# A SwiGLU feed-forward layer on one core: the order and the shape of the first weight loads, and the order of the first matmuls

## The chip, the cores and the metric

The kernel runs on one core of a Trainium2 chip, in one launch. The metric is the time of one execution on the device in microseconds (us). Before the change it is 120.17 us, the median of three runs (119.89 to 120.64). The profile is one further execution, in which the hardware profiler recorded every instruction and every DMA packet.

## What is computed

One sequence of S = 2048 tokens of width D = 512 goes through a gated feed-forward layer with F = 1376 inner columns. All tensors are bf16.

```python
def reference(x, w_gate, w_up, w_down):
    g = _silu(x @ w_gate)
    u = x @ w_up
    return (g * u) @ w_down
```

x is [1, 2048, 512], w_gate and w_up are [512, 1376], w_down is [1376, 512].

## The kernel before

**Tiling.** D is cut into KD = 4 blocks of 128 rows (index dk), which are summed in PSUM. F is cut into ten tiles of 128 columns (ft 0 to 9) and a rest of 96 columns. The tokens are cut into NSC = 4 chunks of SC = 512. The hidden activations are kept transposed, with F on the partitions: for each chunk c and each tile ft there is a group "G" (gate) and a group "U" (up), and each of them fills one PSUM bank of 128 x 512. A group has four steps, one for each dk (`gu_step`), and each step is two matmuls of 64 weight columns, one for the upper and one for the lower half of the array's columns, which run side by side. ScalarE then writes the silu of the gate bank to an fp32 buffer `sg_sb` (four buffers), and VectorE multiplies that with the up bank into `hT_sb`. The rest of F is done in groups "X" (32 of its columns as gate and up, and further 64 as gate) and "Y" (those 64 as up). The second product, groups "O", runs over all tiles of F at the end, mostly in strips of 32 rows (`strips`), and its results are stored tile by tile.

**Order on the engines.** Every engine runs a list that is written out by hand. `plan_tiles` puts gates and ups in the order in which TensorE runs them: for each list in `fts` first all its gates, then all its ups; before the change these lists are [0], [1], [2, 3], [4], ... [9] in every chunk. `s_P` counts the groups that TensorE has finished, in that order, and ScalarE and VectorE wait for these counts. Eight banks are used in turn (`turn` says in which order), so a group waits (`free`) until those who read the group eight places before it are done.

**The opening.** TensorE starts with N_WARM = 6 matmuls of ones, 512 columns wide (`warm`, L359), and N_FILL = 2 fillers (L364), each of two matmuls of 64 rows and 128 columns. Then it waits for `xn`, the first 256 tokens as they lie in memory, and transposes them against the identity matrix (L374, L382). The four results, one for each dk, are copied to `xT_sb` by VectorE and ScalarE in turn. After that come the first gates and ups of chunk 0. The first 256 tokens are taken first (columns 0 to HT = 256 of the bank), since tokens 256 to 511 come later by two transposing DMAs, `x0b` and `x0c`. The order by hand is: gates of tiles 0 and 1 (alternating, dk by dk) and ups of tiles 0 and 1 on 256 tokens; gate 0 on the next 128 and the last 128; then up 0, gate 1 and up 1 on tokens 256 to 511. From tile 2 on a group runs on all 512 tokens at once.

**Loads.** `load_w` (L97) loads columns f0 to f1 of w_gate or w_up for all four dk in one DMA. The columns go by slabs of two tiles, (0, 2), (2, 4), (4, 6), (6, 8), and the last one, (8, 11). A row of such a DMA is 512 bytes long (256 columns), and the last slab's is longer. The slab of gates 0 and 1, `wg0`, is issued from ScalarE's queue (`loads_on_scalar`, L110); all others go from SyncE's queue in this order (`loads_on_sync`, L113): `xn`, `wu0` (ups 0 and 1), `x0b`, `x0c`, then gate and up of each further slab, `wut` (the last 32 columns of w_up), the transposing loads of chunks 1 to 3, w_down (`wd`), four copies of the last 96 rows of w_down on 32 partitions each (`wdt0` to `wdt3`), and `wdl`. A step of TensorE waits for the load that it needs first (`need`), each load having a semaphore of its own.

Of the kernel before, what the change touches and what calls it, by code (L numbers as in the profile page):

```python
# [6 lines left out]
BF16 = mybir.dt.bfloat16  # L7
FP32 = mybir.dt.float32

N_WARM = 6  # L10
N_FILL = 2


def bass_standalone__swiglu_ffn__prompt_kernel(nc, x, w_gate, w_up, w_down, out):
    _, S, D = x.shape
    F = w_gate.shape[1]
    P = 128
    KD = D // P
    NFF = F // P
    NFT = NFF + 1  # L20
# [26 lines left out]
    with ExitStack() as es:  # L47
# [17 lines left out]
        o_sb = [sb(f"o_sb{i}", [P, D], BF16) for i in range(NOS)]  # L65
        psum = ps("psum", [P, NB, 512], FP32)
        banks = [psum[:, i, :] for i in range(NB)]
        turn = [0, 2, 1, 3, 4, 5, 6, 7]

        xn_sb = sb("xn_sb", [P, NXN, D], BF16)  # L70
        ident = sb("ident", [P, P], BF16)
# [22 lines left out]
                xT_sb[:, :, t0:t1], xf[t0:t1, :]  # L94
            ).then_inc(load_sem(name), 16)

        def load_w(eng, name, src, base, f0, f1):  # L97
            eng.dma_start(
                w_sb[:, :, base + f0:base + f1],
                src[:, f0:f1].rearrange("(k p) f -> p k f", p=P),  # L100
            ).then_inc(load_sem(name), 16)

        slabs = [(0, 2), (2, 4), (4, 6), (6, 8), (8, NFT)]
        slab_of = {ft: a for a, b in slabs for ft in range(a, b)}

        def load_slab(eng, a, b):
            load_w(eng, f"wg{a}", w_gate, 0, a * P, min(b * P, F))
            load_w(eng, f"wu{a}", w_up, UPH, a * P, min(b * P, F - 32))

        def loads_on_scalar(act):  # L110
            load_w(act, "wg0", w_gate, 0, 0, slabs[0][1] * P)

        def loads_on_sync(sp):  # L113
            sp.dma_start(
                xn_sb[:, :, :].rearrange("p j d -> p (j d)"), xf[0:HT, :].rearrange("(p j) d -> p (j d)", j=NXN)
            ).then_inc(load_sem("xn"), 16)
            load_w(sp, "wu0", w_up, UPH, 0, slabs[0][1] * P)
            load_x(sp, "x0b", HT, HT + P)
            load_x(sp, "x0c", HT + P, SC)
            for a, b in slabs[1:]:  # L120
                load_slab(sp, a, b)
            load_w(sp, "wut", w_up, F - (F - 32), F - 32, F)
            for c in range(1, NSC):
                load_x(sp, f"x{c}", c * SC, (c + 1) * SC)
            sp.dma_start(
                wd_sb[:, 0:NFF, :], w_down[0:NFF * P, :].rearrange("(k p) d -> p k d", p=P)
            ).then_inc(load_sem("wd"), 16)
            for c in range(NSC):
                sp.dma_start(
                    wdt_sb[R * c:R * (c + 1), :, :], w_down[NFF * P:F, :].rearrange("(q p) d -> p q d", p=R)  # L130
                ).then_inc(load_sem(f"wdt{c}"), 16)
            sp.dma_start(wdl_sb[:, :], w_down[NFF * P:F, LASTA:D]).then_inc(load_sem("wdl"), 16)


# [94 lines left out]
        NT = len(groups)  # L229

        for c in range(NSC):
            for fts in [[0], [1], [2, 3]] + [[ft] for ft in range(4, NFF)]:
                plan_tiles(c, fts)
            plan_x(c)
        for pi in range(NSC // 2):
# [40 lines left out]
            ).then_inc(s_I, 1)  # L276

        def on_scalar(act):
            loads_on_scalar(act)
            act.activation(adummy[:, 0:4], zero_c, ACT.Silu)  # L280
            for op in act_ops:
                act.wait_ge(s_P, op["g"]["at"] + 1)
                if op["kind"] == "silu":
                    if op["free"]:
                        act.wait_ge(s_D, op["free"])
                    fn = ACT.Silu
                else:
                    if op["stored"][1]:
                        act.wait_ge(*op["stored"])
                    fn = ACT.Copy  # L290
                act.activation(op["out"], op["src"], fn).then_inc(s_A, 1)  # L291
            for t, c0, c1, ob, eng, n in stores:
                if (c0, c1) == (0, LASTA):
                    act.wait_ge(s_A, n)
                    act.dma_start(rows_of(t)[:, c0:c1], o_sb[ob][:, c0:c1]).then_inc(s_out[ob], 16)
# [16 lines left out]
        def on_tensor(pe):  # L312
# [19 lines left out]
            def gu_step(g, dk, n0, n1):  # L332
                c, ft = g["c"], g["ft"]
                if c > 0:
                    need(f"x{c}")
                if c == 0 and n1 > HT:
                    need("x0b")
                if c == 0 and n1 > HT + P:
                    need("x0c")
                need(("wg" if g["kind"] == "G" else "wu") + str(slab_of[ft]))  # L340
                if c == 0 and n0 < HT:
                    after(*xt_ready[dk])
                col = (0 if g["kind"] == "G" else UPH) + ft * P
                for m in (0, HC):
                    ins = pe.matmul(  # L345
                        g["bank"][m:m + HC, n0:n1], lhsT=w_sb[:, dk, col + m:col + m + HC],
                        rhs=xT_sb[:, dk, c * SC + n0:c * SC + n1], start=(dk == 0), stop=(dk == KD - 1),
                        tile_position=(0, m),
                    )
                if n1 == SC and dk == KD - 1:  # L350
                    ins.then_inc(s_P, 1)
# [30 lines left out]
                    ins = pe.transpose(tview_last()[m:m + HC, i, :], xn_sb[:, i, c0:c0 + HC], ident[:, :])  # L382
            ins.then_inc(s_P, 1)

            g0, u0, g1, u1 = groups[NT:NT + 4]
            for dk in range(KD):
                for g in (g0, g1):
                    gu_step(g, dk, 0, HT)
            for g in (u0, u1):
                gu_matmuls(g, 0, HT)  # L390
            gu_matmuls(g0, HT, HT + P)
            gu_matmuls(g0, HT + P, SC)
            for g in (u0, g1, u1):
                gu_matmuls(g, HT, SC)

            for g in groups[NT + 4:]:
                kind = g["kind"]
                if kind == "O":
                    break
                free(g)  # L400
                if kind in "GU":
                    gu_matmuls(g, 0, SC)
                elif kind == "X":
                    c = g["c"]
                    need(f"wg{slab_of[NFF]}")
                    need("wut")
                    for dk in range(KD):
                        for m in (0, HC):
                            ins = pe.matmul(  # L409
                                g["bank"][m:m + HC, :], lhsT=w_sb[:, dk, XC0 + m:XC0 + m + HC],  # L410
                                rhs=xT_sb[:, dk, c * SC:(c + 1) * SC],
                                start=(dk == 0), stop=(dk == KD - 1), tile_position=(0, m),
                            )
                    ins.then_inc(s_P, 1)
                elif kind == "Y":
                    need(f"wu{slab_of[NFF]}")
                    for dk in range(KD):
                        for c in (2 * g["pi"], 2 * g["pi"] + 1):
                            y0, y1 = yblk(c)
                            ins = pe.matmul(  # L420
                                g["bank"][y0:y1, :], lhsT=w_sb[:, dk, YC0:YC0 + 64],
                                rhs=xT_sb[:, dk, c * SC:(c + 1) * SC],
                                start=(dk == 0), stop=(dk == KD - 1),
                                tile_position=(0, y0), skip_group_check=True,
                            )
                    ins.then_inc(s_P, 1)
# [119 lines left out]
```

## Time and profile before

| | us |
|---|---|
| median of three runs | 120.17 |
| lowest and highest run | 119.89, 120.64 |
| the profiled execution | 120.67 |
| its span, first to last instruction | 119.3 |
| TensorE busy within the span | 116.6 |
| VectorE busy | 43.4 |
| ScalarE busy | 35.5 |
| SyncE's DMA queue, share of 16 engines | 27.1% |

The span is shorter than the execution's own time by 1.3 us, which lie before the first and behind the last instruction. Busy times of TensorE are to be read with care: a matmul's record runs from its start until its last result is written, so records of neighbours overlap, and a busy engine isn't one at full rate. How many matmuls of a shape start within a stretch tells the rate. A "DMA issue" is the instruction on the queue of SyncE (SPq) or ScalarE (ACTq); the time to landing counts from there to the last increment of the load's semaphore. The stretch that the change touches looks like this in the page's 40 slices of about 3 us each, from the left (tenths of busy time, then GB/s of all DMAs):

```
PE   7999999999999999999999999999999999999993
DVE  0103534442534452444352444369800040214331
ACT  4225243265242365232454323470000030213001
DMA  3999999991000000000000000000000023023612
GB/s 80 278 283 335 194 253 228 269 295 23 0 5 0 0 0 0 5 0 5 0 5 0 0 0 0 5 0 0 5 0 5 0 86 95 0 92 106 204 44 88
```

All weights and tokens are loaded in the first 29 us or so; the stores come at the end.

### The profile page before, as it was taken

What the parts mean: (1) busy time and instruction counts of PE and PEld (TensorE: products, weight loads), DVE (VectorE), ACT (ScalarE), POOL (GpSimd) and SP (SyncE); (2) the same over time, 40 slices, a digit from 0 to 9 for tenths busy, and PEclk for the clock granted to TensorE, in tenths of its full rate; (3) what the DMA queues carried; (4) which work ended last, traced back from release to release, by engine and by line L of the source; (5) the groups of instructions that cost most, each with busy time, mean ns of one, the idle gap of its engine ahead of it and who ended that gap; (6) DMA issues with size and microseconds to landing.
All of it is one profiled execution on the core that took longest, in us unless ns stands there. A gap on an engine that the chain in (4) does not pass through costs nothing.

```text
span 119.3 us, 2992 instructions
## 1 busy us (share of the span) xinstructions
PE 116.6 (98%) x1343; PEld 66.4 (56%) x1344; DVE 43.4 (36%) x68; ACT 35.5 (30%) x61; POOL 0.4 (0%) x5
## 2 busy tenths in 40 slices
PE   7999999999999999999999999999999999999993
PEld 2796555555555555555555555554444444464452
DVE  0103534442534452444352444369800040214331
ACT  4225243265242365232454323470000030213001
POOL 1000000000000000000000000000000000000000
DMA  3999999991000000000000000000000023023612
GB/s 80 278 283 335 194 253 228 269 295 23 0 5 0 0 0 0 5 0 5 0 5 0 0 0 0 5 0 0 5 0 5 0 86 95 0 92 106 204 44 88
DMA packets 17596, 8.92 MB, mean 75 GB/s; under 512 B 8624, under 2 KB 17456, under 8 KB 17584
## 3 DMA queue, kind: packets, MB, share of 16 engines
q1 hardware_dynamic: 16912, 8.38, 27.1%
q10 hardware_dynamic: 672, 0.36, 1.0%
q8 instruction: 10, 0.16, 0.6%
q14 instruction: 2, 0.02, 0.0%
HBM read 4.81 MB, written 2.10 MB: 58 GB/s over the span
## 4 chain that ended last, share of the span: by engine, by line
PE 98%; issue 0%; DVE 0%
PE psum L345 59%; PE psum L456 24%; PE psum L433 7%; PE psum L409 3%; PE psum L359 2%; PE psum L420 1%; PE psum L382 0%; PE psum L374 0%; PE psum L364 0%; DVE o_sb L309 0%; PE psum L508 0%
## 5 line engine op out<-in xcount | busy, mean ns | idle before, releaser
L345 PE MATMUL psum<-xT_sb,w_sb 128*64 128x512 bf16 (+2 forms) x680 | 71.0, 371 | 0.0
L345 PEld LDWEIGHTS psum<-xT_sb,w_sb 128*64 128x64 bf16 x680 | 43.0, 112 | 27.1
L305 DVE TENSOR_TENSOR hT_sb<-sg_sb,psum 128x512 bf16<-128x512 f32 x40 | 27.5, 687 | 41.5 <-PE psum L345 36.6
L291 ACT ACTIVATE sg_sb<-psum 128x512 f32<-128x512 f32 x40 | 23.8, 596 | 41.6 <-PE psum L345 41.6
L456 PE MATMUL psum<-wd_sb,hT_sb 32*128 32x512 bf16 x480 | 26.9, 374 | 0.0
L456 PEld LDWEIGHTS psum<-wd_sb,hT_sb 32*128 32x128 bf16 x480 | 13.0, 93 | 13.0 <-issue 0.4
L309 DVE CAST o_sb<-psum 128x512 bf16<-128x512 f32 (+1 forms) x11 | 6.4, 603 | 25.2 <-PE psum L456 19.9
L291 ACT ACTIVATE o_sb<-psum 128x512 bf16<-128x512 f32 (+1 forms) x7 | 3.7, 580 | 33.0 <-PE psum L456 25.9
L433 PE MATMUL psum<-wd_sb,hT_sb 128*128 128x512 bf16 (+2 forms) x59 | 8.7, 307 | 0.2 <-issue 0.2
L433 PEld LDWEIGHTS psum<-wd_sb,hT_sb 128*128 128x128 bf16 x60 | 4.6, 98 | 4.6 <-issue 0.4
L305 DVE TENSOR_TENSOR ht_sb<-sgy_sb,yu_sb 32x512 bf16<-32x512 f32 x8 | 5.5, 683 | 0.4
L409 PE MATMUL psum<-xT_sb,w_sb 128*64 128x512 bf16 x32 | 4.2, 379 | 0.0
L305 DVE TENSOR_TENSOR ht_sb<-sgx_sb,psum 32x512 bf16<-32x512 f32 x4 | 2.8, 691 | 3.5 <-ACT sgx_sb L291 3.5
L291 ACT ACTIVATE sgx_sb<-psum 32x512 f32<-32x512 f32 x4 | 2.4, 588 | 4.5 <-PE psum L409 4.5
L359 PE MATMUL psum<-const-bfloat16-1.0 128*128 128x512 bf16 x6 | 2.7, 623 | 0.8 <-PEq L531 0.8
L456 PE MATMUL psum<-wdt_sb,ht_sb 32*128 32x512 bf16 (+1 forms) x48 | 3.3, 371 | 0.0
L409 PEld LDWEIGHTS psum<-xT_sb,w_sb 128*64 128x64 bf16 x32 | 2.0, 110 | 1.4
L291 ACT ACTIVATE sgy_sb<-psum 64x512 f32<-64x512 f32 x4 | 2.4, 590 | 0.1
L456 PEld LDWEIGHTS psum<-wdt_sb,ht_sb 32*128 32x128 bf16 x48 | 1.3, 93 | 1.3
L420 PE MATMUL psum<-xT_sb,w_sb 128*64 128x512 bf16 x16 | 1.9, 379 | 0.0
L359 PEld LDWEIGHTS psum<-const-bfloat16-1.0 128*128 128x128 bf16 x6 | 0.7, 133 | 1.9 <-issue 1.9
L280 ACT ACT_TABLE_LOAD x1 | 1.3, 1283 | 1.2 <-PEq L531 1.2
(21 smaller groups left out, 7.6 us busy)
## 6 DMA issues: line engine op xcount, KB each, us to landing
out_dram<-o_sb SPq DMA_DIRECT2D x15, 128.0 KB, 1.8
wd_sb<-in_w_down_dram SPq DMA_DIRECT2D x1, 1280.0 KB, 8.9
w_sb<-in_w_up_dram SPq DMA_DIRECT2D x4, 256.0 KB, 4.0
w_sb<-in_w_gate_dram SPq DMA_DIRECT2D x3, 256.0 KB, 3.9
wdt_sb<-in_w_down_dram SPq DMA_DIRECT2D x4, 96.0 KB, 7.2
w_sb<-in_w_gate_dram SPq DMA_DIRECT2D x1, 352.0 KB, 6.2
w_sb<-in_w_up_dram SPq DMA_DIRECT2D x1, 320.0 KB, 6.3
w_sb<-in_w_gate_dram ACTq DMA_DIRECT2D x1, 256.0 KB, 3.6
```

Source lines behind the costliest of these rows:

```text
L280: act.activation(adummy[:, 0:4], zero_c, ACT.Silu)
L291: act.activation(op["out"], op["src"], fn).then_inc(s_A, 1)
L305: ins = dve.tensor_tensor(op["out"], op["a"], op["b"], ALU.mult)
L309: ins = dve.tensor_copy(op["out"], op["src"])
L345: ins = pe.matmul(g["bank"][m:m + HC, n0:n1], lhsT=w_sb[:, dk, col + m:col + m + HC], rhs=xT_sb[:, dk, c * SC + n0:c * SC + n1], start=(dk ...
L359: pe.matmul(banks[NB - 1][:, 0:width], lhsT=ones_w, rhs=ones_m[:, 0:width], start=True, stop=True)
L409: ins = pe.matmul(g["bank"][m:m + HC, :], lhsT=w_sb[:, dk, XC0 + m:XC0 + m + HC], rhs=xT_sb[:, dk, c * SC:(c + 1) * SC], start=(dk == 0), ...
L420: ins = pe.matmul(g["bank"][y0:y1, :], lhsT=w_sb[:, dk, YC0:YC0 + 64], rhs=xT_sb[:, dk, c * SC:(c + 1) * SC], start=(dk == 0), stop=(dk == ...
L433: ins = pe.matmul(g["bank"][:, 0:c1 - c0], lhsT=hT_sb[:, fk, t * P:(t + 1) * P], rhs=wd_sb[:, fk, c0:c1], start=(start and fk == 0), stop= ...
L456: ins = pe.matmul(g["bank"][:, 0:c1 - c0], lhsT=h(r, g["t"]), rhs=w[R * r:R * (r + 1), c0:c1], start=(start and n == 0), stop=final, tile_ ...
```

## The change

The first slab of gates and ups now has four tiles, 0 to 3, and comes in four DMAs: gates for dk 0 and 1 (`wg0a`), gates for dk 2 and 3 (`wg0b`), and the ups likewise (`wu0a`, `wu0b`). Each of them moves 256 KB, in rows of 1 KB (512 columns). All four go from SyncE's queue right behind `xn`, and ScalarE's queue issues no load any more. `wdt0` follows them, ahead of `x0b` and `x0c`; the other three copies stay where they were. The further slabs are (4, 8) and (8, 11), so fewer and larger DMAs follow.

TensorE runs five warm-up matmuls and four fillers. Behind the transposes come, on the first 256 tokens: gates 0 and 1 for dk 0 and 1, gates 2 and 3 for dk 0 and 1, then the same for dk 2 and 3; then ups 0 to 3 one after another for dk 0 and 1, and again for dk 2 and 3. Then gate 0 on the next 128 and the last 128 tokens, and gates 1 to 3 and ups 0 to 3 on tokens 256 to 511. In chunk 0 the plan begins with the four gates and then the four ups; all other tiles, in all chunks, go one by one, gate and up. The banks are taken in plain order.

```diff
-N_WARM = 6
-N_FILL = 2
+N_WARM = 5
+N_FILL = 4
...
-        turn = [0, 2, 1, 3, 4, 5, 6, 7]
+        turn = list(range(NB))
...
-        def load_w(eng, name, src, base, f0, f1):
+        def load_w(eng, name, src, base, f0, f1, k0=0, k1=KD):
             eng.dma_start(
-                w_sb[:, :, base + f0:base + f1],
-                src[:, f0:f1].rearrange("(k p) f -> p k f", p=P),
+                w_sb[:, k0:k1, base + f0:base + f1],
+                src[k0 * P:k1 * P, f0:f1].rearrange("(k p) f -> p k f", p=P),
             ).then_inc(load_sem(name), 16)
...
-        slabs = [(0, 2), (2, 4), (4, 6), (6, 8), (8, NFT)]
+        slabs = [(0, 4), (4, 8), (8, NFT)]
+        KH = KD // 2
+        n_first = slabs[0][1]
...
-        def loads_on_scalar(act):
-            load_w(act, "wg0", w_gate, 0, 0, slabs[0][1] * P)
+        def load_strip(eng, c):
+            eng.dma_start(
+                wdt_sb[R * c:R * (c + 1), :, :], w_down[NFF * P:F, :].rearrange("(q p) d -> p q d", p=R)
+            ).then_inc(load_sem(f"wdt{c}"), 16)
...
-            load_w(sp, "wu0", w_up, UPH, 0, slabs[0][1] * P)
+            load_w(sp, "wg0a", w_gate, 0, 0, n_first * P, 0, KH)
+            load_w(sp, "wg0b", w_gate, 0, 0, n_first * P, KH, KD)
+            load_w(sp, "wu0a", w_up, UPH, 0, n_first * P, 0, KH)
+            load_w(sp, "wu0b", w_up, UPH, 0, n_first * P, KH, KD)
+            load_strip(sp, 0)
             load_x(sp, "x0b", HT, HT + P)
             load_x(sp, "x0c", HT + P, SC)
...
-            for fts in [[0], [1], [2, 3]] + [[ft] for ft in range(4, NFF)]:
+            for fts in [list(range(n_first if c == 0 else 1))] + [
+                [ft] for ft in range(n_first if c == 0 else 1, NFF)
+            ]:
                 plan_tiles(c, fts)
...
         def on_scalar(act):
-            loads_on_scalar(act)
...
-                need(("wg" if g["kind"] == "G" else "wu") + str(slab_of[ft]))
+                half = ("a" if dk < KH else "b") if ft < n_first else ""
+                need(("wg" if g["kind"] == "G" else "wu") + str(slab_of[ft]) + half)
...
-            g0, u0, g1, u1 = groups[NT:NT + 4]
-            for dk in range(KD):
-                for g in (g0, g1):
-                    gu_step(g, dk, 0, HT)
-            for g in (u0, u1):
-                gu_matmuls(g, 0, HT)
-            gu_matmuls(g0, HT, HT + P)
-            gu_matmuls(g0, HT + P, SC)
-            for g in (u0, g1, u1):
+            gates, ups = groups[NT:NT + n_first], groups[NT + n_first:NT + 2 * n_first]
+            for dks in (range(KH), range(KH, KD)):
+                for a in range(0, n_first, 2):
+                    for dk in dks:
+                        for g in gates[a:a + 2]:
+                            gu_step(g, dk, 0, HT)
+            for dks in (range(KH), range(KH, KD)):
+                for g in ups:
+                    for dk in dks:
+                        gu_step(g, dk, 0, HT)
+            gu_matmuls(gates[0], HT, HT + P)
+            gu_matmuls(gates[0], HT + P, SC)
+            for g in gates[1:] + ups:
                 gu_matmuls(g, HT, SC)
```

## The prediction

> **What bounds the kernel now.** I read the page's busy row and its chain of waits first, to see whether any engine but TensorE sets the end.
>
> ```profile
> PE 116.6 (98%) x1343; PEld 66.4 (56%) x1344; DVE 43.4 (36%) x68; ACT 35.5 (30%) x61; POOL 0.4 (0%) x5
> ...
> PE 98%; issue 0%; DVE 0%
> ```
>
> TensorE never waits once it runs, so a load or an eviction matters only if it makes TensorE wait or start later. The change touches the first 13 us, so I then read the chain in order of time (start, us, what) up to 30 us.
>
> ```profile
> 0.77 2.72 PE psum L359 x6
> 3.49 0.33 PE psum L364 x3
> 3.82 0.33 PE psum L374 x11
> 4.15 0.36 PE psum L382 x4
> 4.51 18.56 PE psum L345 x200
> 23.07 0.86 PE psum L409 x8
> ```
>
> Warm-up (L359), fillers (L364), transposes (L374, L382), then gates and ups without a break. The timeline puts the first gate matmul at 4.42 and the first transpose at 3.65. A busy row doesn't tell the rate, so I asked for the matmuls by shape in two stretches, 4.42 to 6.84 and 7.76 to 9.06 (count, busy us, mean ns):
>
> ```profile
> L345 PE MATMUL psum<-xT_sb,w_sb 128*64 128x256 bf16 x24 | 2.6, 408 | 0.0
> ```
>
> ```profile
> L345 PE MATMUL psum<-xT_sb,w_sb 128*64 128x256 bf16 x24 | 1.5, 273 | 0.0
> ```
>
> A step of gate or up is two matmuls side by side, one per half of the columns. Twelve pairs 256 wide take 2.42 us in the first stretch (0.20, the last one still running) and 1.30 us in the second (0.108): TensorE begins at half rate and later doubles it, though the page's granted clock is 1.00 throughout. When it turned follows from the sum: from 4.42 to 9.07 stand 28 pairs of 256 columns and 8 of 128, which at full rate are 28 x 0.108 + 8 x 0.056 = 3.47 us. They took 4.65. The 1.18 us of excess are 11 pairs at double time, so the rate doubled at about 4.42 + 11 x 0.213 = 6.8, some 6.0 us after the first warm-up matmul. This 1.2 us is the largest thing that an opening could still win.
>
> Last, what starts the gates: the DMA issues by window (KB, us to landing), and their issue times in the timeline.
>
> ```profile
> w_sb<-in_w_gate_dram ACTq DMA_DIRECT2D x1, 256.0 KB, 3.6
> xn_sb<-in_x_dram SPq DMA_DIRECT2D x1, 256.0 KB, 2.9
> w_sb<-in_w_up_dram SPq DMA_DIRECT2D x1, 256.0 KB, 4.0
> ```
>
> ```profile
> 0.73 0.46 ACTq L98 DMA_DIRECT2D w_sb<-in_w_gate_dram  x1
> 0.74 0.41 SPq L114 DMA_DIRECT2D xn_sb<-in_x_dram  x1
> 1.20 0.41 SPq L98 DMA_DIRECT2D w_sb<-in_w_up_dram  x1
> 1.67 2.57 SPq L93 DMA_TRANSPOSE xT_sb<-in_x_dram  x2
> 4.28 0.58 SPq L98 DMA_DIRECT2D w_sb<-in_w_gate_dram  x1
> ```
>
> xn lands at 0.74 + 2.9 = 3.6 and the transposes follow at 3.65. wg0 lands at 0.73 + 3.6 = 4.3 and the first gate follows at 4.42. Those two landings hold the opening; wu0 at 5.2 is in time.
>
> **The change, part by part.**
>
> *Warm-up and fillers.* One warm-up matmul less is -0.43 us (the L359 weight loads in the timeline stand 0.43 apart), two fillers more are 2 x 0.107 = +0.21 (half of a 256 pair at half rate). TensorE is free for the transposes at about 3.4 instead of 3.6; what comes last there is xn.
>
> *wg0 leaves ScalarE's queue.* xn loses its companion. By 2.9 us 0.22 of its 0.26 MB had moved and wg0 was beginning; the last 0.04 MB alone at the 325 GB/s of 2.4 to 2.8 take 0.13 us. I bound xn's gain by 0 and 0.25 us (3.35, just before the fillers end) and take 0.15. ScalarE's table load moves up; it is idle until 4.09, so nothing comes of it.
>
> *wg0a.* 256 KB as wg0, second on SyncE's queue, issued at 1.20 instead of 0.73. Worst: it keeps 3.6 us from issue and lands at 4.8. Best: with xn's bytes done by 3.05, 0.75 us of transfer and 0.3 to the landing (an estimate, from xn's 3.05 and 3.35 above), 4.1. Nearest row: wu0 holds exactly this place, lands at 5.2 behind one more 256 KB DMA; less that one (0.7 to 0.77) it is 4.45. Between it and the best I take 4.3. The first gate stands at 4.3 then, -0.1 (bounds -0.25, the transposes' own gain, and +0.5).
>
> *What an earlier start is worth.* If the doubling stays at 6.8, time moved before it is done at half rate and saves half: -0.05 (bounds -0.13, +0.25). If the doubling moved along, it would be the whole -0.1. I take the half: three runs of this kernel, with the same loads, lie 0.75 us apart, so the doubling doesn't seem tied to the start.
>
> *Rows of 1 KB.* Two windows give rates (columns: stretch, then busy times, clock, DMA share, GB/s): the slabs' 512 B rows, and w_down's 1 KB rows.
>
> ```profile
> 7.60:10.00 2.40, 2.40 (x47) 2.04 (x43) 1.13 (x2) 1.19 (x2) 0.00 (x0) 1.00 1.15 340
> ...
> 23.60:24.60 1.00, 1.00 (x12) 0.57 (x10) 0.19 (x1) 0.61 (x2) 0.00 (x0) 1.00 1.07 375
> ```
>
> 256 KB then take 0.70 us instead of 0.77. The Trainium skill ("DMA: Bandwidth & Descriptors", Specifications) gives 512 B as the least transfer for line rate, so the wider rows would gain nothing; the trace has a tenth between them. By the page each piece would land 0.07 us later than I say, inside the slack below.
>
> *Do the pieces come in time?* With wg0a at 4.3: wg0b 5.0, wu0a 5.7, wu0b 6.4, strip 0 (96 KB) 6.7, x0b and x0c (0.56 and 0.45 apart in this trace) 7.2 and 7.7. Eight pairs use one piece. With the doubling at 6.8, TensorE wants wg0b at 4.3 + 8 x 0.213 = 6.0, wu0a at 7.2, wu0b at 8.1, x0b at 9.0: slack of 1.0 us and more. In a run whose rate doubles before the first gate they are wanted at 5.2, 6.0, 6.9, 7.8, 8.0: slack of 0.2 to 0.6. No wait either way. On SyncE's queue strip 0 adds one issue (0.46) ahead of two transposes (1.3 each); slab 4-7's gates go out at about 6.1 and land, 3.7 after that and twice as large, by 10.5, wanted at 12.5; its ups by 11.5, wanted at 13.4. The transposes of x1 are issued at about 9.6 (now 10.14), land at about 17 and are wanted at 23.75. w_down is wanted near 80.
>
> *Width.* F tiles 2 and 3 change 16 pairs of 512 columns (1.72 us between two silus for 8 pairs, 0.215) into 32 of 256: 32 x 0.108 - 16 x 0.215 = +0.02 (bounds 0, +0.06).
>
> *Banks and evictions.* Gate 0 completes at 9.4; four silus at 596 ns end at 11.9. Up 0 completes at 11.1; four products at 687 ns end at 14.0. Gate 4 wants gate 0's bank at 12.5 (read by 10.1), gate 6 wants up 0's at 15.9 (read by 11.9), the silu of gate 4 wants its buffer at 13.3 (free at 11.9). Nothing waits. Without this slack of 1.4 us every late eviction would be TensorE's. The plain order of banks, single tiles in the later chunks and the moved wdt0 cost nothing, for TensorE has no idle time behind 4.42 that they could cause or remove while a bank is reused eight groups later as now.
>
> *Sum.* Profiled execution: span 119.34 and 1.33 around it, 120.67. Change: -0.05 + 0.02 = -0.03. That run is 0.5 us above the median; on the median, **120.1 us**.
>
> **The rivals.**
>
> *Slower: the half rate lasts longer.* Place: the gap between the last transpose (now ending near 4.3, then 4.1) and wg0a. For it: wg0a is issued 0.47 us later, TensorE may stand idle 0.2 to 0.7 us where it now stands 0.12, and the doubling comes only after long activity. Price: if that idle time makes the activity start over, 6.0 us from 4.3 put the doubling at 10.3 instead of 6.8; 3.5 us at half rate cost 1.75, so 121.9 (121.2 if only the part of the warm-up before 3.4 is lost, 2.0 to 2.6 us of delay). It decides from a gap longer than the 0.14 us that this trace has between warm-up and fillers without harm. Against it: such gaps are short beside 6 us. The Trainium skill ("TensorE: Matmul & The Clock Gate", Part 1, What's actually happening) has the rate set by a free-running window of 3.4 us, so that a short gap costs nothing unless the window falls short of busy; the trace agrees so far as 6.0 us lie between one and two windows. By that rule the doubling also stays where it falls when the start moves, as I took it.
>
> *Faster.* Start at its best bound and a doubling before the first gate: 120.67 - 0.25 - 1.18 + 0.02 = 119.3. For it: runs of one kernel already lie between 119.89 and 120.64, which a doubling at different times would give. Against: that luck belongs to the run, not to the change. Only with something unseen does it pass 119.0.
>
> *No effect on the first gate.* xn was not slowed by wg0, and wg0a lands as wg0 did: 120.2, within the forecast's range. A late piece under an early doubling, 0.2 to 0.6 us, gives 120.5.
>
> **How the numbers follow.** Forecast 0.65, own range 119.4 to 120.9 (start -0.13 to +0.25, and the spread of the runs); no effect or a late piece 0.05; faster 0.12, of it 0.06 under 119.0; slower 0.18, nearly all beyond 121.4. One per cent of 120.17, about what a measurement of this kernel can tell from no change, is 119.0 to 121.4: faster 0.06, within 0.76, slower 0.18. A range of 119.2 to 121.3 leaves out that 0.06 and some 0.14 of the slower case.
>
> **What would show it.** xn landing at 3.35 to 3.6 and the first transpose just behind; wg0a at 4.1 to 4.8 and the first L345 matmul within 0.1 us of it; no idle time of TensorE from there to x0c; twelve 256 pairs in 1.30 us wherever the rate has doubled, and that point near 6 to 7 us; a silu of gate 0 near 9.4 and no wait of gate 4. A first gate after 4.9, a wait on wu0a or x0b, or a doubling after 8 us would make the prediction wrong.

## The result and the profile after

| | before | after |
|---|---|---|
| median of 14 runs, us | 120.01 | 120.81 |
| lowest and highest | 119.50, 120.64 | 120.38, 121.53 |
| ratio of the runs, with its 95% interval | | 1.0072 (1.0044 to 1.0100) |
| profiled execution, and its span | 120.67, 119.3 | 121.53, 120.2 |

The change makes the kernel slower by 0.7%, or 0.8 us, clear of the noise. The time lies inside the predicted range, but the forecast was no change (-0.03 us). The profiled execution of after shares the highest time of its 14 runs, and that of before (120.67) lies above all 14 of its own. In the section on the experiments ratios and mean spans leave out, as slow, each run more than 1.5% above its kernel's fastest (one of e2's eleven, one of e6's twelve, three of e4's six), while medians hold all.

The page's busy row and the chain of after:

```profile
PE 116.4 (97%) x1379; PEld 71.2 (59%) x1379; DVE 43.2 (36%) x68; ACT 35.1 (29%) x61; POOL 0.4 (0%) x5
...
PE 87%; DMA 6%; SPq 5%; issue 1%; DVE 0%
```

The chain, which was all TensorE before, now runs through a DMA and through SyncE's queue. In order of time (start, us, what) it shows which:

```profile
6.32 0.59 SPq L98
6.91 0.05 issue
6.96 7.12 DMA w_sb<-in_w_up_dram
14.08 0.14 issue
14.21 9.69 PE psum L353 x88
```

The ups of tiles 4 to 7 are issued at 6.96 and land 7.12 us later, at 14.08; all work behind 14.21 hangs on that landing. Steps of TensorE start in the trace at 12.69 and then at 14.22, where a step takes 0.22: TensorE stands still for 1.3 us. The list of waits shows what remains of it behind the end of the last matmul's record (total, times, longest):

```profile
PE psum L353 <- DMA w_sb<-in_w_up_dram: 1.1, 1, 1.1
```

What came late was the last bit of this load. A load raises its semaphore in 16 parts, and the trace has the time of each: 15 of the 16 had landed by 12.30, which is 0.6 us before TensorE wanted the load, and the last one came 1.78 us behind them.

The opening itself went as forecast in this execution. By the timeline the first transpose starts at 3.40 and the first gate at 4.20 (before: 3.65 and 4.42).

```profile
3.40 0.53 PE L382 MATMUL psum<-ident,xn_sb 64*128 64x64 bf16 x12
3.85 0.43 PE L390 MATMUL psum<-ident,xn_sb 128*64 128x128 bf16 x4
4.20 2.00 PE L353 MATMUL psum<-xT_sb,w_sb 128*64 128x256 bf16 x18
```

The rate, by matmul form from 4.20 to 5.90 and from 6.20 to 8.50 (count, busy us, mean ns):

```profile
L353 PE MATMUL psum<-xT_sb,w_sb 128*64 128x256 bf16 x17 | 2.0, 410 | 0.0
```

```profile
L353 PE MATMUL psum<-xT_sb,w_sb 128*64 128x256 bf16 x46 | 2.7, 273 | 0.0
```

The mean of 410 ns has become 273 by 6.2: the rate doubles near 6.0 here, where it doubled at 6.8 in the profile of before. Without the 1.3 us of standstill the span would be 118.9, 0.44 under the profile of before: half of the 0.22 us of earlier start and half of the 0.8 us of earlier doubling are 0.5. So the profile alone would put the whole loss on one late load. The experiments put a part of it there, 0.28 to 0.53 of 0.87 us.

### The profile page after: what moved, and what is told of

Read it like the earlier page. It is cut to its first block, busy times and chain, and to the rows that moved or that the text cites. A ratio compares the mean times of both kernels' runs of the same rounds, so it can differ in the third digit from the quotient of the medians.

```text
span 120.2 us, 3060 instructions
## 1 busy us (share of the span) xinstructions
PE 116.4 (97%) x1379; PEld 71.2 (59%) x1379; DVE 43.2 (36%) x68; ACT 35.1 (29%) x61; POOL 0.4 (0%) x5
## 4 chain that ended last, share of the span: by engine, by line
PE 87%; DMA 6%; SPq 5%; issue 1%; DVE 0%
PE psum L353 51%; PE psum L468 24%; PE psum L445 7%; DMA w_sb<-in_w_up_dram 6%; PE psum L421 3%; SPq L93 2%; SPq L98 2%; PE psum L432 1%; SPq L113 0%; SPq L118 0%; DVE o_sb L316 0%; PE psum L520 0%
## 5 line engine op out<-in xcount | busy, mean ns | idle before, releaser
L353 PEld LDWEIGHTS psum<-xT_sb,w_sb 128*64 128x64 bf16 x712 | 47.7, 112 | 23.5 <-ACT sg_sb L298 1.6
L421 PEld LDWEIGHTS psum<-xT_sb,w_sb 128*64 128x64 bf16 x32 | 2.2, 110 | 1.2
```

The source lines that it names most:

```text
L353: ins = pe.matmul(g["bank"][m:m + HC, n0:n1], lhsT=w_sb[:, dk, col + m:col + m + HC], rhs=xT_sb[:, dk, c * SC + n0:c * SC + n1], start=(dk ...
L421: ins = pe.matmul(g["bank"][m:m + HC, :], lhsT=w_sb[:, dk, XC0 + m:XC0 + m + HC], rhs=xT_sb[:, dk, c * SC:(c + 1) * SC], start=(dk == 0), ...
```

## The experiments

All times in this section are of TensorE's span from the first to the last instruction or of the whole run; "mean span" is the mean over a kernel's runs, set against the mean span of the kernel before in runs made along with it (118.5 to 118.65). With twelve runs such a difference is uncertain by 0.10 to 0.15 us (one standard error; 0.15 to 0.27 where there are six runs, and 0.56 for e4), and the difference between two of these kernels by 0.13 to 0.19, so a step of 0.2 us from one to another is not clear of noise. For the changed kernel the same difference is 120.88 - 120.01 = 0.87 us, from the means of its run times.

| kernel | median, us | ratio to before (95%) | mean span less before's |
|---|---|---|---|
| the changed kernel | 120.81 | 1.0072 (1.0044 to 1.0100) | 0.87 |
| e1_two_tile_slabs | 120.52 | 1.0058 (1.0035 to 1.0080) | 0.59 |
| e2_gates_4_5_first | 120.65 | 1.0056 (1.0034 to 1.0078) | 0.68 |
| e3_strip_back | 120.59 | 1.0075 (1.0047 to 1.0104) | 0.88 |
| e4_slab_on_act | 127.09 | 1.0503 (1.0431 to 1.0574) | 6.2 |
| e6_opening_only | 120.64 | 1.0052 (1.0030 to 1.0074) | 0.48 |
| e7_tokens_before_ups | 120.25 | 1.0020 (0.9996 to 1.0045) | 0.23 |
| e8_pieces_by_tiles | 120.35 | 1.0048 (1.0023 to 1.0074) | 0.53 |
| e10_opening_six_two | 120.23 | 1.0034 (1.0005 to 1.0063) | 0.26 |
| e13_tokens_first_six_two | 120.10 | 1.0018 (0.9991 to 1.0046) | 0.10 |
| e15_tokens_first_gates_4_5 | 120.09 | 1.0029 (1.0009 to 1.0050) | 0.30 |
| e14_after_more_fillers | 120.82 | 1.0083 (1.0055 to 1.0112) | 0.92 |
| e16_after_fillers | 121.44 | 1.0129 (1.0085 to 1.0173) | 1.64 |
| e5_before_wide_slab | 120.40 | 1.0044 (1.0019 to 1.0069) | 0.53 |
| e9_before_five_four | 120.15 | 1.0005 (0.9975 to 1.0036) | 0.14 |
| e11_before_fillers | 120.43 | 1.0043 (1.0018 to 1.0067) | 0.36 |
| e12_before_three_two | 120.98 | 1.0114 (1.0071 to 1.0157) | 1.18 |

### The late slab: four runs on the changed kernel

```diff
-        slabs = [(0, 4), (4, 8), (8, NFT)]
+        slabs = [(0, 4), (4, 6), (6, 8), (8, NFT)]
```

> The changed kernel with slabs (4, 6), (6, 8) again in place of (4, 8); the opening stays. Theory: the 1.3 us that TensorE stands before up 4 are the change's whole loss, because up 4 waits for the last byte of 512 KB. Then the ups of tiles 4 and 5 (256 KB) land before 11.5 us, up 4 follows gate 4 without a gap, and the time is 119.6 to 119.9, a little under the kernel before (the first gate stands 0.2 us earlier). Rival, the half rate at the start (the prediction's slower case): the time stays near 120.8 though the wait is gone. Rival, the queue runs dry behind the transposes whatever the slab: the ups still land after 12.5 and some of the gap stays.

The ups of tiles 4 and 5 landed at 11.2, no gate or up waited for them, and the profile has no standstill of TensorE behind the first gate. But the median fell by 0.3 only, not by 1.0. In the profile of the changed kernel the wait is plain, yet it is not the whole loss; neither theory alone had this right.

```diff
-            for fts in [list(range(n_first if c == 0 else 1))] + [
-                [ft] for ft in range(n_first if c == 0 else 1, NFF)
-            ]:
+            for fts in (
+                [list(range(n_first)), [4, 5]] + [[ft] for ft in range(6, NFF)] if c == 0
+                else [[ft] for ft in range(NFF)]
+            ):
```

> The changed kernel; in chunk 0 the gates of tiles 4 and 5 both run before their ups, all loads as they are. Up 4 is then wanted 0.86 us later, near 13.8. Theory (the wait on the ups of slab 4 to 7 is the loss): the load lands where it did, 13 to 14.1, and the gap shrinks to 0 to 0.4; time 119.7 to 120.2. Rival, half rate: no change from 120.8. Rival, the gap has to do with banks or evictions: it moves but stays 1.3 us.

The ups landed at 13.4 and up 4, now wanted 0.86 us later, didn't wait in the profile (span 119.1). The mean span is 0.68 above before instead of 0.87, again far from the whole, and that gain of 0.2 is no more than its uncertainty.

```diff
-            load_strip(sp, 0)
...
-            for c in range(1, NSC):
+            for c in range(NSC):
                 load_strip(sp, c)
```

> The changed kernel with the first strip of w_down back behind w_down. It takes one issue of 0.51 us and 96 KB from in front of the transposes. Theory, late issue: the slab of tiles 4 to 7 goes out 0.5 us earlier, its ups land 0.5 us earlier and the median falls by 0.3 to 0.5 to 120.3 to 120.5. Theory, one DMA engine is held up by the instruction fetch (16 KB, near 11.3 us, just while those ups are under way): the landing stays at 13 to 14, the time near 120.8, unless the ups are through before the fetch.

The slab's ups were issued 0.5 us earlier and landed at 11.73, 1.48 behind its gates: they were nearly through when the instruction fetch of that execution began (11.34), and the load behind them was the late one. Behind the first gate nothing waits in the profile (span 119.3 with a doubling near 6.7, which is the profile of before less 0.07). Still the seven runs are no faster than the changed kernel within their uncertainty. The strip's place alone is not shown to matter.

```diff
-            for a, b in slabs[1:]:
+            for a, b in slabs[2:]:
                 load_slab(sp, a, b)
...
-            for op in act_ops:
+            for n_op, op in enumerate(act_ops):
+                if n_op == KD // 2:
+                    load_slab(act, *slabs[1])
```

> The changed kernel with the slab of tiles 4 to 7 (gates, then ups) issued from ScalarE's queue behind its second copy to xT_sb, near 4.7 and 5.3 us, in place of 6.3 and 7.0 from SyncE's. Theory, late issue: the queue does not run dry behind the transposes, the ups land near 11 and up 4 does not wait; 119.6 to 120.0. Against: from 5.8 on these 1 MB share the engines with wu0b, x0b and x0c, which may come 0.5 to 1 us later and make TensorE wait near 7.5 to 8.5; then 120.2 to 120.8. Half rate: 120.8 in any case.

Far worse than any theory had it. The slab's loads were under way together with the transposing loads, and x0b and x0c, which land at 7.7 and 8.2 in the changed kernel, landed at 9.95 and 12.70. This execution shows two things more. Its rate had doubled before the first gate (4.11 by the trace's record of the clock, the first gate at 4.22), and there TensorE already waits for a piece of the opening that was issued before ScalarE's loads (waits from 4 to 8 us):

```profile
PE psum L355 <- DMA w_sb<-in_w_up_dram: 0.3, 1, 0.3
```

That is wu0a, wanted at 6.05 and landed at 6.46; by starts TensorE loses 0.45 us. And its granted clock moves within the trace (columns from the left: stretch, then busy times, the granted clock, DMA share, GB/s):

```profile
4.11:10.94 6.83, 4.45 (x76) 3.49 (x72) 0.18 (x1) 0.55 (x2) 0.00 (x0) 1.00 1.11 270
10.94:17.76 6.82, 5.02 (x52) 4.28 (x54) 0.76 (x2) 2.39 (x4) 0.00 (x0) 0.50 1.16 216
```

TensorE waits twice for tokens, from 8.3 to 10.0 and from 10.3 to 12.7, and the clock is halved from 10.94 to 17.76. The changes stand 6.83 us apart, twice 3.41. The Trainium skill ("TensorE: Matmul & The Clock Gate", Part 1, What's actually happening) gives a free-running window of 3413 ns, and the trace agrees. The same page of the Trainium skill (Why this matters for your kernels) asks for no idle gaps of more than about 3 us between bursts of matmuls; here two gaps, neither that long, were enough to halve the clock, with 2.1 us of idle time in the last 3.4 us before 10.94 (busy 1.32 of 3.41).

### Is it the opening? Four runs that split it

The floor of the runs is a clue. The kernel before often reaches a span of 118.2, which is its profile's 119.34 less the 1.18 us of half rate: in these runs the rate would have doubled before the first gate. There is no trace of such a run of before, but the profile of e13 below, of the same span, has it so. None of e1, e2, e3 falls below 118.7.

e6_opening_only joins the edits of e1 and e3.

> The changed kernel with slabs of two tiles and the strip back behind w_down: of the change only the opening is left (four pieces by halves of D ahead of x0b and x0c, the new order of matmuls, 5 warm-up matmuls and 4 fillers). Theory A, late pieces: in runs whose rate doubles early TensorE uses a piece in 0.87 us while the pieces land 1.0 apart, so the span cannot fall under the landing of x0c + 0.05 + 110.12: with x0c at 8.2 to 8.4 a lowest span of 118.4 to 118.6 (before 118.2), in runs with a late doubling nothing is lost; median 120.0 to 120.2. Theory B, the rate doubles later than before because less full-width work stands ahead of it: the whole distribution shifts by 0.2 to 0.5, spans up to 119.7; median 120.2 to 120.5.

Measured: lowest span 118.7, highest 119.5, mean 0.48 above before. The opening alone costs about half of what the whole change costs. The floor is near theory A's (118.4 to 118.6), but the median of 120.64 lies above what either theory had.

e7_tokens_before_ups is e6 with the order of loads and matmuls changed:

```diff
-            load_w(sp, "wu0a", w_up, UPH, 0, n_first * P, 0, KH)
-            load_w(sp, "wu0b", w_up, UPH, 0, n_first * P, KH, KD)
             load_x(sp, "x0b", HT, HT + P)
             load_x(sp, "x0c", HT + P, SC)
+            load_w(sp, "wu0a", w_up, UPH, 0, n_first * P, 0, KH)
+            load_w(sp, "wu0b", w_up, UPH, 0, n_first * P, KH, KD)
...
-            for dks in (range(KH), range(KH, KD)):
-                for g in ups:
-                    for dk in dks:
-                        gu_step(g, dk, 0, HT)
             gu_matmuls(gates[0], HT, HT + P)
             gu_matmuls(gates[0], HT + P, SC)
-            for g in gates[1:] + ups:
+            for g in gates[1:]:
                 gu_matmuls(g, HT, SC)
+            for dks in (range(KH), range(KH, KD)):
+                for g in ups:
+                    for dk in dks:
+                        gu_step(g, dk, 0, SC)
```

> As e6_opening_only, but x0b and x0c are issued ahead of the ups, and TensorE runs the four gates on all tokens before the four ups. A piece of tokens (256 KB) makes 16 pairs of work where a piece of weights makes 8. Theory A: no piece is late even with an early doubling, the lowest span falls to 118.0 to 118.2 and the median to 119.7 to 119.9. Theory B: it keeps the time of e6_opening_only, within 0.1.

The mean fell by 0.25 (uncertain by 0.13) to 0.23 above before, the lowest span from 118.7 to 118.4: theory A's direction, and about half of its size.

e9_before_five_four and e10_opening_six_two exchange the warm-up alone, one in the kernel before, one in e6 (there the other way round):

```diff
-N_WARM = 6
-N_FILL = 2
+N_WARM = 5
+N_FILL = 4
```

> The kernel before with nothing changed but 5 warm-up matmuls and 4 fillers instead of 6 and 2. Theory A: no loss, 119.8 to 119.9, since loads and order are those of before and the first gate stays within 0.1 us of 4.4. Theory B: TensorE has 0.43 us less of full-width work before 3.3 us; the doubling comes up to 0.9 us later on average, the median rises by 0.2 to 0.5 and single spans reach 119.5 to 119.7, which the kernel before never shows (119.3 at most).

> As e6_opening_only, with 6 warm-up matmuls and 2 fillers as before. The first transpose stands at 3.65 and the first gate near 4.4, 0.2 later than in e6_opening_only. Theory A: as e6_opening_only or 0.1 slower. Theory B: 0.2 to 0.4 faster than e6_opening_only, with spans of 119.4 at most.

e9 is 0.14 above before, with single spans of 119.4 at most, and its interval holds no change. e10 is 0.22 below e6. So both theories may hold a part: taking the longer warm-up back (e10) gains about as much as moving the tokens forward (e7). But e10's gain is uncertain by 0.15, and e9 has none of the spans of 119.5 to 119.7 that theory B expected.

### What doubles the rate

e11 and e12 change the warm-up of the kernel before by more than the change did.

```diff
-N_WARM = 6
-N_FILL = 2
+N_WARM = 1
+N_FILL = 20
```

> The kernel before with 1 warm-up matmul and 20 fillers: TensorE is as busy ahead of the transposes (to 3.5 us) and the first gate stays near 4.4, but nearly all of it is pairs of 64 rows and 128 columns. If full-width work is what brings the doubling (theory B), it comes up to 2 us later: mean span 119.2 to 119.7, single spans to 120.3. If any work counts: 118.65 as before, at most 119.3.

```diff
-N_WARM = 6
+N_WARM = 3
```

> The kernel before with 3 warm-up matmuls and 2 fillers: TensorE is idle for 1.3 us more ahead of the transposes, the loads and the first gate as before. If the doubling needs a certain amount of work before it (theory B, now by idle time): up to 1.3 us later, mean span 119.0 to 119.4, single spans to 119.9. If only the time since the first matmul counts: 118.65, at most 119.3.

With fillers the rate doubles early in the one profile: already from 4.9 to 6.3 us a gate's matmul has a mean of 283 ns.

```profile
L345 PE MATMUL psum<-xT_sb,w_sb 128*64 128x256 bf16 x30 | 2.0, 283 | 0.0
```

With 1.3 us of idle time the rate is still half from 4.39 to 7.7 us, and the record of the clock has it doubled at 8.26; all six spans are 119.4 or more. The list of waits has 1.1 of the 1.3 us, behind the end of the last filler's record:

```profile
PE psum L374 <- DMA xn_sb<-in_x_dram: 1.1, 1, 1.1
```

The matmuls of the first stretch:

```profile
L345 PE MATMUL psum<-xT_sb,w_sb 128*64 128x256 bf16 x32 | 3.6, 420 | 0.0
```

So it is idle time ahead of the doubling that delays it, and not the width of the work: theory B holds for idle time and falls for fillers (e11's highest span is 119.4, where the theory had up to 120.3). In the change five warm-up matmuls and four fillers end at 3.40 by their starts, instead of 3.6; where xn lands at 3.6, as in e9 and e7, TensorE idles 0.25 us that it was busy before. That so short a gap also delays the doubling isn't shown by itself.

By its profile e11 has lost its 0.36 for another reason, and this is the clue to the late slab. In its chain (start, us, what) stands a load that the kernel before doesn't wait for, the ups of tiles 2 and 3:

```profile
4.91 5.50 DMA w_sb<-in_w_up_dram
10.41 0.04 issue
10.45 3.64 PE psum L345 x31
```

They land at 8.6 in the kernel before, and here at 10.41. With 62 matmuls and weight loads more in front, the first refill of instructions, the "instruction fetch" of the expectations (one packet of 16 KB, 0.95 us long, on a queue of its own that the trace calls "instruction"), came at 8.20 instead of 10.45. The trace doesn't say whose instructions these are; that they are TensorE's is inferred. In the changed kernel it stands in the list of DMA queues from 11.25 to 12.3 us (packets, MB, share of 16 engines):

```profile
q8 instruction: 1, 0.02, 5.6%
```

### The instruction fetch

The same holds in seventeen of the eighteen profiles: one load that is issued but not landed when this packet begins comes late, 1.9 to 3.1 us after it. (In e4, with loads on two queues at once, it is 3.6 us.) It need not be the next one to land: in the kernel before gates 6 and 7 still came at 10.92, and the ups behind them were late. From the packets and landings of the traces, in us, for nine of the seventeen:

| kernel | fetch begins | late load | lands | after the fetch |
|---|---|---|---|---|
| before | 10.45 | ups 6, 7 | 13.07 | 2.6 |
| e11_before_fillers | 8.20 | ups 2, 3 | 10.41 | 2.2 |
| e5_before_wide_slab | 11.04 | ups 4 to 7 | 13.30 | 2.3 |
| e1_two_tile_slabs | 10.74 | gates 6, 7 | 13.37 | 2.6 |
| e6_opening_only | 9.16 | gates 6, 7 | 12.26 | 3.1 |
| after | 11.28 | ups 4 to 7 | 14.08 | 2.8 |
| e2_gates_4_5_first | 10.85 | ups 4 to 7 | 13.41 | 2.6 |
| e14_after_more_fillers | 10.52 | ups 4 to 7 | 13.36 | 2.8 |
| e16_after_fillers | 7.87 | x0b | 9.78 | 1.9 |

In sixteen of them 15 of the late load's 16 parts came with the stream and the last one trailed by 0.7 to 2.2 us: in e11 the fifteenth landed at 8.23 and the last at 10.41, in the kernel before at 11.63 and 13.07. (In e16 two parts trailed.) This fits a packet that holds up one of the 16 DMA engines; which engine carried it, the trace doesn't say.

In the kernel before the victim is a small slab that is wanted 3 us later. e5 puts the wide slab alone into it:

```diff
-        slabs = [(0, 2), (2, 4), (4, 6), (6, 8), (8, NFT)]
+        slabs = [(0, 2), (2, 4), (4, 8), (8, NFT)]
```

> The kernel before with (4, 6) and (6, 8) joined to (4, 8): the change's wide slab alone, in the opening of before. Up 4 is wanted at 13.4 when the rate doubles at 6.8 and at 12.2 when it doubles before the first gate. If the 512 KB of ups are through before the instruction fetch (near 10 us) or are held up by it only to 12.5, the loss is 0 to 0.2 in the mean span; if they land at 13.3 to 14 as in the changed kernel, up 4 waits in nearly every run and the mean span rises by 0.5 to 1.0 from 118.65.

```profile
6.01 7.28 DMA w_sb<-in_w_up_dram
13.30 0.14 issue
13.43 6.63 PE psum L345 x59
```

The wait is there in an opening that is otherwise that of before, and the wide slab by itself costs 0.53 us (uncertain by 0.10): the one part of the loss that a single run shows well clear of noise.

Whether it is the size or the fetch was asked by moving the fetch in the changed kernel, first with 3 warm-up matmuls and 12 fillers, then with 1 and 20:

> The changed kernel with 3 warm-up matmuls and 12 fillers in place of 5 and 4: TensorE is as busy up to 3.47 us, but has 28 instructions more behind it, so its instruction fetch (16 KB, in the changed kernel at 11.28, while the ups of slab 4 to 7 were under way) should come at 9 to 10, while that slab's gates are under way. Theory, fetch: whatever load is under way lands 2.2 to 3 us after the fetch begins; then the gates of the slab land at 11.3 to 12.3, the ups at 12.4 to 12.9 instead of 14.1, up 4 waits at most 0.4, and the mean span falls from 119.5 to 119.1 to 119.3. Theory, size alone (512 KB simply takes that long): the ups land at 13.5 to 14 and the mean span stays at 119.5.

> The changed kernel with 1 warm-up matmul and 20 fillers, since 3 and 12 moved the fetch by 0.8 us only, to 10.5, still into the ups. With 56 instructions more than the changed kernel the fetch should begin at 8.5 to 9.7, while the gates of slab 4 to 7 are under way (they land at 11 in all runs so far). Theory, fetch: those gates then land at 11.3 to 12.2 and the ups at 12.3 to 12.8, before or just when up 4 is wanted; mean span 119.1 to 119.3 against 119.5. Theory, size alone: the ups land at 13.3 to 14 as before and the mean span stays at 119.5.

In e14 the fetch began at 10.52, where the gates were nearly through (10.79), and hit the ups again; the run tells nothing apart. Nor is it shown that the fillers moved it there: in kernels with the changed kernel's own list of TensorE instructions (e1, e3, e4, e6) it began anywhere from 9.16 to 11.46. In e16 it came at 7.87, earlier than meant, and hit the transposing loads: x0b landed at 9.78, and TensorE waited twice for tokens. What the DMA engines moved meanwhile (last column):

```profile
8.25:9.75 1.50, 0.62 (x12) 0.34 (x8) 0.00 (x0) 0.00 (x0) 0.00 (x0) 1.00 0.81 25
9.75:12.25 2.50, 2.21 (x46) 2.05 (x48) 0.00 (x0) 1.34 (x3) 0.00 (x0) 1.00 1.07 358
```

For 1.5 us there is almost nothing, then 358 GB/s. The wide slab, whose own parts were not held up this time, landed at 11.77 (gates) and 13.11 (ups), 1.34 us apart; in the changed kernel it was 11.19 and 14.08, 2.9 apart. At 1.34 the ups would have landed at 12.5 there (an estimate), before up 4 wanted them near 12.9. The time of e16 didn't fall as was expected, because the fetch found another victim, and its ups landed between what the two theories had. But e3's profile agrees with it (1.48 apart), and so do the parts of the late load (15 of 16 by 12.30). So the size makes 1.3 to 1.5 us of the distance and the fetch 1.4 to 1.6, and the standstill in the profile of the changed kernel needs both: e1, with the fetch and small slabs, and e3, with the wide slab and a later fetch, don't have it.

### The shape of the pieces, and all terms together

e8_pieces_by_tiles is e6 with pieces of two tiles and all four dk:

```diff
-            load_w(sp, "wg0a", w_gate, 0, 0, n_first * P, 0, KH)
-            load_w(sp, "wg0b", w_gate, 0, 0, n_first * P, KH, KD)
+            load_w(sp, "wg0a", w_gate, 0, 0, 2 * P)
+            load_w(sp, "wg0b", w_gate, 0, 2 * P, n_first * P)
```

(the ups likewise, and TensorE takes two tiles at a time)

> As e6_opening_only, but the four pieces are two tiles wide and hold all four dk (rows of 512 bytes), and TensorE goes through them two tiles at a time. Theory, the pieces are late because of where they stand (four of them ahead of the tokens), not because of their rows: they land within 0.2 us of those of e6_opening_only and its mean span of 119.1 stays within 0.15. Theory, the halves of D in 1 KB rows are what is slow: the pieces land 0.75 apart, x0c before 7.8, and the mean span falls to 118.8 to 118.9.

0.53 above before against 0.48, a difference well under its uncertainty of 0.17: that the rows of 1 KB and the halves of D help or hurt is not shown. In its profile the four pieces land at 4.43, 5.77, 6.60, 7.35, x0c at 8.45; in that of e6 at 4.17, 5.01, 6.30, 7.01, x0c at 8.10. So the shape of the pieces is not what makes them late; four of them stand ahead of the tokens in both.

e13 is e7 with 6 warm-up matmuls and 2 fillers; e15 is e13 with the order of e2.

> As e7_tokens_before_ups (slabs of two tiles, the strip back, x0b and x0c ahead of the ups, four gates on all tokens first), with 6 warm-up matmuls and 2 fillers. If late pieces and the shorter warm-up are all that is left of the change's loss, the mean span comes back to 118.5 to 118.8 (before 118.65; e7_tokens_before_ups 118.88), with a lowest span of 118.1 to 118.3. If something else in the order of four gates and four ups costs time, it stays at 118.9 or above.

> As e13_tokens_first_six_two, with the gates of tiles 4 and 5 ahead of their ups, so that up 4 is wanted 0.86 us later and a load held up by the instruction fetch is covered. Expected: no wait anywhere from the first gate on, lowest span 118.1 to 118.2, mean span 118.5 to 118.7 against 118.6 before: no loss left, and no gain that can be measured.

e13 comes back to within 0.10 us of the kernel before, its interval holds no difference, and its lowest span of 118.24 is the profiled one, which doubled before the first gate (3.76 by the record of the clock, the first gate at 4.39). e15 missed its expectation: it is 0.30 above before, and its interval (1.0009 to 1.0050) leaves out no change. Its profile waits 0.3 us for wu0a, which lands at 8.28 and is now issued behind 2.6 us of transposes' issues. Whether this wait is the whole of the 0.30 is open; in e13's profile wu0a landed at 7.70 and nothing waited for it. No kernel beat the one before.

## Why the prediction was wrong

**The step that failed is "Do the pieces come in time?"**, which ended in "No wait either way".

- *The slab of tiles 4 to 7* was put down as "by 10.5, wanted at 12.5; its ups by 11.5, wanted at 13.4". Its issue at 6.32 was nearly right (6.1 forecast). It landed at 11.19 and 14.08, and up 4 wanted it at 12.9, so that TensorE stood for 1.3 us. Two things were left out. The first is that the slab is issued only behind the issues of both transposes, and by then little was on its way: the engines ran at 151 GB/s from 7.5 to 9.7, as they had done at 135 from 5.4 to 6.8 before (last column, GB/s; after first, then before):

```profile
7.50:9.70 2.20, 2.20 (x53) 2.20 (x50) 0.00 (x0) 0.51 (x2) 0.00 (x0) 1.00 0.81 151
9.70:11.20 1.50, 1.50 (x32) 1.50 (x30) 0.26 (x1) 1.50 (x4) 0.00 (x0) 1.00 1.06 374
```

```profile
5.40:6.80 1.40, 1.40 (x18) 1.39 (x16) 0.00 (x0) 0.00 (x0) 0.00 (x0) 1.00 0.80 135
```

  The second is that the ups fell into the instruction fetch, and their last part came 1.78 us behind the others. The trace of before showed both: ups 6 and 7 landed 2.15 us after the gates 6 and 7, where their neighbours were 0.74 apart, and I read over it. Price: 0.3 to 0.5 us (e1 and e6 against the changed kernel, each uncertain by nearly 0.2, and e5 against before, 0.53).
- *The pieces of the opening* were taken 0.7 us apart at 375 GB/s, a rate from another stretch. They landed at 4.14, 5.04, 6.13, 7.09, that is 1.0 apart, and x0b and x0c at 7.66 and 8.19 (7.2 and 7.7 forecast). In a late doubling, which is all that the profile of before showed, the slack covers it, and one execution agrees with the forecast: e3's profile, with the doubling where before's was, lies 0.07 under it (-0.03 forecast). That is partly luck, as its fetch missed the slab. In an early one a piece is used in 0.87 us, and wu0a was given a slack that it doesn't have: it was to land at 5.7 and be wanted at 6.0, and in the ten profiles in which it is the third of four pieces ahead of the tokens it landed at 6.1 to 7.2. e4's profile, the only one of them that doubles before the first gate, loses 0.45 us to it. How common an early doubling is, spans of 118.2 to 118.3 suggest: about a third of the kernel before's. Price: 0.15 to 0.25 us (e7 against e6, e13 against e10), which is one to two times its uncertainty. The wider rows, for which I took the trace against the Trainium skill's 512 B ("DMA: Bandwidth & Descriptors", Specifications), made no difference that can be told (e8: 0.05 us, uncertain by 0.17), as the page has it.
- *Warm-up and fillers* were reckoned as time only. They also keep TensorE busy until xn comes, and e12 shows that idle time there, 1.3 us of it, delays the doubling. The slower rival had this mechanism but put the gap between the transposes and wg0a and gave it 1.75 us. For the change's own warm-up it was some 0.13 to 0.22 us (e10 and e6, e13 and e7, e9 and before all have the same sign, each near its own uncertainty).

Taking the parts back one after another, the loss goes from 0.87 over 0.48 (wide slab and strip, e6) and 0.26 (warm-up, e10) to 0.10 (tokens ahead of the ups, e13). These steps of 0.39, 0.22 and 0.16 and the 0.10 left make the 0.87 by the way they are taken, which is no check of them, and each is uncertain by 0.12 to 0.2. What is shown is that the three together are the loss, as e13 is not to be told from before, and that the wide slab alone costs 0.53 (e5). How the rest divides between the warm-up and the order of the loads is open.

That 120.81 lies inside the range is owed to the range, which had to hold the spread of the runs, and not to the account. The rival that came nearest, a late piece under an early doubling at 120.5, shared a chance of 0.05 with no effect and was meant for the pieces of the opening, not for the slab.

**What was right.** wg0a landed at 4.14 (4.3 forecast), the first gate stood at 4.20 in the profile (4.3), the 256-wide matmuls kept their rate (273 ns), and no bank or buffer waits. The evictions were as reckoned, silu of gate 0 at 9.2. xn landed 0.36 earlier in this profile, outside its bounds of 0 to 0.25; but in the thirteen profiles in which ScalarE's queue no longer issues wg0 it landed anywhere from 3.22 to 3.71, on average at 3.43, against 3.58 in the five with the old opening, and these 0.15 us are the forecast's. That an earlier start is worth half as long as the rate is half fits the profile's 0.44 but was not tested by itself.

**What stays open.** Why the first packet of instructions comes when it does, 7.9 to 11.9 us in these kernels, was not settled. The two kernels with the most instructions ahead have it earliest (e16 at 7.87, e11 at 8.20), but the same list of TensorE has it at 9.16 in e6 and at 11.46 in e4. Why one part of the load then often trails by more than the packet's own 1 us is not explained. No profile of e6 or of the changed kernel itself with an early doubling was taken; their waits there are read from e4's profile and from the floor of their spans.

## What to carry to other kernels

A kernel whose TensorE never waits in the profile can still be a few tenths of a microsecond from waiting, and the profile shows one of several openings: check the slack of each load for the earliest clock that the spread of the runs allows, not for the one in the trace. Ask of each load how much work it makes: here 256 KB of tokens made twice as many matmuls as 256 KB of weights, and putting the tokens ahead of the second half of the weights gained 0.16 to 0.25 us, little more than the uncertainty. And join loads only where the landing of the last byte has some 2 us to spare, because a fetch of instructions can fall into any of them.

## What the runs showed of the hardware

- Around the first 16 KB packet of instructions one load came late in seventeen of eighteen profiles, 1.9 to 3.1 us after the packet began, and in sixteen of these it was the last of its 16 parts that trailed (by 1.78 us in the changed kernel). With transposing loads under way almost all traffic stopped for 1.5 us (25 GB/s, e16).
- With loads on ScalarE's queue beside them, the transposing loads of SyncE's queue came late: x0c landed at 12.7 instead of 8.2 (e4).
- The rate of the matmuls doubled anywhere between 3.7 (e15, by the clock record) and 8.3 us (e12) after the span's start, and fell back to half after 2.1 us of idle time within 3.4 us (e4).
